# Attention and two expert layers on one core: the last pair's scalings moved ahead of the weight passes, and a woven group's relu moved ahead of the second half's exponentials

## The chip, the core and the metric

The kernel runs on one core of a Trainium2 chip. The time is the device time of one execution in microseconds (us); the less, the better. The engines that matter are TensorE (PE: matmuls, PEld: loads of their stationary operand), VectorE (DVE), ScalarE (ACT) and SyncE's queue of transfers (SP). Each engine runs its instructions in program order and waits on semaphores of the others.

## What is computed

Three steps follow each other. The attention has 2 batches x 12 heads of 448 rows with 64 columns, and its mask makes it causal. The two layers after it work on 896 tokens, 768 wide inside the model and 2048 wide in the middle.

```python
scores = scale * np.matmul(q, k.transpose(0, 1, 3, 2))
scores = np.where(mask, -1000000000.0, scores)
scores = scores - np.max(scores, axis=-1, keepdims=True)
attn = np.exp(scores)
attn = attn / (np.sum(attn, axis=-1, keepdims=True) + 1e-09)
attn_out = np.matmul(attn, v)
...
h = np.maximum(x @ w_in, 0.0)        # first layer, x from attn_out
x = (h * h @ w_out)
...
h = x @ w_in                         # second layer
g = h - np.tanh(h)
out = (g @ w_out)
```

## The kernel before, in words

**Number format.** The weights come as 64-bit words. Each unit of weights (128 x 768) is turned into two 32-bit parts by steps that alternate between engines. DVE shifts (L115), ACT scales the upper words (L105), DVE merges (L120) and sets the sign (L125), ACT rounds the result to the upper part (L127), and DVE takes the difference as the lower part (L134 or L136, in turn). After this last step, called split, SP loads the unit three further on (L98), since there are three raw buffers. The split results go into a ring of 8 buffers. Each product of the layers is then three matmuls: upper x upper, upper x lower, lower x upper (L370, L371, L372). Only the third reads the lower part of the weights.

**Attention.** The 24 heads are done as 12 pairs (`NPAIR`), numbered 0 to 11. The loop over `s` is a software pipeline: in step `s`, pair `s` gets its scores, row maxima (DVE, L296 and L298) and exponentials (ACT, L305); pair `s-1` gets the reciprocals of its row sums (DVE, `recips`) and the first of its scalings (DVE, `norms`, L317); and pair `s-2` gets the rest of its scalings, its transposes (PE, L323), the copies of these out of PSUM (ACT, `tcopy`, L329) and the product with V (PE, `pv`, L341). The result of pair `s-3` is taken out of PSUM by ACT (`xhi`, L354) and DVE (`xlo`, L358). The seven row blocks of a pair, 0 to 6, are 64 to 448 columns wide. Scores and exponentials come in two halves; `exps(s, e1[:-1])` are the exponentials of the second half. A pair's transposes go in four groups, 0 to 3, through two PSUM buffers, so that groups 2 and 3 can only be written once ACT has copied groups 0 and 1. In steps 12 and 13 there are no scores left, only the last pairs.

**Woven groups.** From step 8 on the first batch of pairs is complete, and each step weaves one group of the first layer's matmuls (18 matmuls into one PSUM buffer `h`, called from `fill`) between the attention's. There are six (`EARLY`), in steps 8 to 13, for weight units 0 to 5. At the end of its step `relus` turns the group into its activation: ACT computes relu out of PSUM (L387), squares (L388) and rounds to the upper part (L380). In the next step `relu_lows` has DVE take the lower part (L383). There is one buffer `h` for these groups: the next group cannot start before the relu has read the last one.

**Order.** The order on each engine is the order of the code. The steps of the weight preparation lie in a list `todo`; `one()` takes the next one if the budget of the step (`budget`, in nanoseconds of DVE time) is not used up, and `pump()` takes as many as the budget allows. What they leave for ACT is kept back in `act_late` and put out by `late()`. In steps 12 and 13 the budget is `SHARE_LAST`. After the loop come the rest of the first layer and the second, the weight passes, paced by other budgets.

Of the kernel before, what the change touches and what calls it, by code (L numbers as in the profile page):

```python
# [14 lines left out]
AF = mybir.ActivationFunctionType  # L15
# [12 lines left out]
NPAIR = B * NP  # L28
# [6 lines left out]


SHARE_PAIR = (800, 3300)
SHARE_LAST = 6000
SHARE_HIDDEN = (2400, 500)
SHARE_OUT = 4000  # L40

# [23 lines left out]
def body(ctx: ExitStack, tc: tile.TileContext, qT, kT, vL, w1, w2, w3, w4, out):  # L65
    nc = tc.nc
# [12 lines left out]
    def tmp(name, which="t"):  # L79
        return sb.tile([P, S], F32, tag=f"tmp{which}", bufs=4 if which == "t" else 3, name=name)  # L80
# [72 lines left out]
    def room():  # L153
        i = len(taken) - RING
        return i < 0 or taken[i] < freed[0]
# [10 lines left out]
    def late():  # L166
        while act_late:
            act_late.pop(0)()

    def one():  # L170

        if todo and budget[0] > 0 and (room() or not todo[0][3]):
            take()
            return True

    def take():
        f, cost, _, _ = todo.pop(0)
        f()
        budget[0] -= cost
# [6 lines left out]
    def pump():  # L186
        while one():
            pass
# [29 lines left out]
    def warm(count):  # L218
        o = ps.tile([P, 512], F32, tag="h", bufs=1, name="warm")[:, :S]
        for _ in range(count):  # L220
            nc.tensor.matmul(o, lhsT=ones[:, :P], rhs=ones, start=True, stop=True)
# [6 lines left out]
    for j in range(2):  # L228
        for i in range(2):
            r = maskb[D * j : D * j + D, i]  # L230
# [32 lines left out]
    def scores(n, t):  # L263
        q, k = qk[n]
        banks = []
        for z, cs in enumerate(step(n, t)):
            bank = ps.tile([P, 512], F32, tag="s", bufs=4, name=f"s{n}_{t}_{z}")
            banks.append(bank)
            for c in cs:
                sc[n, c] = bank[:, SOFF[c] : SOFF[c] + D * (c + 1)]  # L270
        for i in range(2):
            for z, cs in enumerate(step(n, t)):
                for c in cs[i : i + 1]:
                    for j in range(2):
                        r, e = slice(D * j, D * j + D), D * (j ^ z)
                        nc.tensor.matmul(sc[n, c][e : e + D], lhsT=q[r, D * c : D * c + D], rhs=k[r, : D * (c + 1)], start=(c == cs[0]), stop=False, skip_group_check=True)  # L276
        for z, cs in enumerate(step(n, t)):
            d = [SOFF[c] // D + c for c in cs]
            o = banks[z].rearrange("p (b k) -> p b k", k=D)[:, d[0] : d[-1] + 1 : max(d[-1] - d[0], 1)]
            for j in range(2):  # L280
                r, e = slice(D * j, D * j + D), D * (j ^ z)
                nc.tensor.matmul(o[e : e + D], lhsT=identb[r, r], rhs=maskb[r, : len(cs)], start=False, stop=True, skip_group_check=True)
        if t == 1:
            qk.pop(n)
            load_qk(n + 3)

    def blocks(n, t):
        return [c for cs in step(n, t) for c in cs]

    def maxes(n, t):  # L290
        if t == 0:
            stat[n] = sb.tile([P, 3, 8], F32, tag="stat", bufs=4, name=f"st{n}")
        st = stat[n]
        cs = blocks(n, t)
        for c in reversed(cs):
            nc.vector.tensor_reduce(out=st[:, 0, SI[c] : SI[c] + 1], in_=sc[n, c], axis=AX.X, op=ALU.max, negate=True)  # L296
        a, z = SI[cs[0]], SI[cs[-1]] + 1
        nc.vector.tensor_scalar_mul(out=st[:, 0, a:z], in0=st[:, 0, a:z], scalar1=0.125)  # L298

    def exps(n, cs):  # L300
        st = stat[n]
        for c in cs:
            w = D * (c + 1)
            i = SI[c]
            nc.scalar.activation(prob[n % 3][:, POFF[c] : POFF[c] + w], sc.pop((n, c)), AF.Exp, bias=st[:, 0, i : i + 1], scale=0.125, accum_out=st[:, 1, i : i + 1])  # L305

    def recips(n):
        st = stat[n]
        nc.vector.tensor_scalar_add(out=st[:, 1, :NQ], in0=st[:, 1, :NQ], scalar1=1e-9)
        nc.vector.reciprocal(out=st[:, 2, :NQ], in_=st[:, 1, :NQ])  # L310

    def norms(n, cs):
        st = stat[n]
        for c in cs:
            i = SI[c]
            p = prob[n % 3][:, POFF[c] : POFF[c] + D * (c + 1)]
            nc.vector.tensor_scalar_mul(out=p, in0=p, scalar1=st[:, 2, i : i + 1])  # L317

    def transposes(n, t):
        bank = tb[n, t] = ps.tile([P, 512], F32, tag="t", bufs=2, name=f"t{n}_{t}")  # L320
        for i, (kc, c) in enumerate(TBLK[4 * t : 4 * t + 4]):
            o = bank.rearrange("p (i j q) -> p i j q", j=2, q=D)[:, i, :: -1 if c in TURNED else 1]
            nc.tensor.transpose(o, prob[n % 3][:, POFF[c] + P * kc : POFF[c] + P * kc + P], ident)  # L323

    def tcopy(n, t):
        if t == 0:
            pt[n] = slot(3 + n % 2, [P, 16, P], F32, f"pt{n}")
        bank = tb.pop((n, t))
        nc.scalar.copy(out=pt[n][:, 4 * t : 4 * t + 4], in_=bank.rearrange("p (i q) -> p i q", q=P))  # L329
# [22 lines left out]
    def xhi(n):  # L352
        b, hp = divmod(n, NP)
        nc.scalar.copy(out=x[hp][:, 0, b], in_=ob[n][:, :S])  # L354

    def xlo(n):
        b, hp = divmod(n, NP)
        nc.vector.tensor_sub(out=x[hp][:, 1, b], in0=ob.pop(n)[:, :S], in1=x[hp][:, 0, b])  # L358
# [20 lines left out]
    def hi_of(dst, v):  # L379
        nc.scalar.copy(out=dst[0], in_=v)  # L380
# [4 lines left out]
    def relu2(h, dst):  # L385
        r = tmp("r")
        nc.scalar.activation(r, h, AF.Relu)  # L387
        nc.scalar.activation(r, r, AF.Square)  # L388
        hi_of(dst, r)
        return r  # L390
# [72 lines left out]
    def early(count):  # L463
        for m in range(count):
            dst = gdst(0, 0, m, 0)
            h = ps.tile([P, 512], F32, tag="h", bufs=1, name=f"h{m}_0")[:, :S]
            for k, _ in enumerate(first_pieces(0, 0, m, 0, h)):
                if k == KD - 1:
                    done.append((h, dst))
                yield  # L470

    done = []
    lows = []
    early_groups = early(EARLY)

    def fill(count):
        for _ in range(count):
            next(early_groups, None)

    def relus():  # L480
        while done:
            h, dst = done.pop(0)
            lows.append((dst, relu2(h, dst)))

    def relu_lows():
        while lows:
            lo_of(*lows.pop(0))
# [34 lines left out]
    for s in range(NPAIR + 2):  # L522
        p, a = s - 1, s - 2
        ss, sp, sa = s < NPAIR, 0 <= p < NPAIR, a >= 0
        f = s - 2 >= NP
        if ss:
            budget[0] = min(budget[0], 0) + (SHARE_PAIR[f] if s > 1 else 0)
            e0, e1 = blocks(s, 0)[::-1], blocks(s, 1)
        else:
            budget[0] = min(budget[0], 0) + SHARE_LAST  # L530
        if sp:
            exps(p, blocks(p, 1)[-1:])
        if ss:
            scores(s, 0)
        if sa:
            norms(a, (3, 5, 6))
        if a >= 1:
            xhi(a - 1)
        if f:
            relu_lows()  # L540
            one()
            fill(1)
        if sa:
            transposes(a, 0)
            tcopy(a, 0)
            transposes(a, 1)
            tcopy(a, 1)
        late()
        if f:
            fill(2)  # L550
        if ss:
            maxes(s, 0)
        if a >= 1:
            xlo(a - 1)
        if f:
            one()
        if ss:
            exps(s, e0[:2])
        if sp:
            recips(p)  # L560
            norms(p, (0, 1, 2))
        if f:
            one()
        if ss:
            scores(s, 1)
        if f:
            fill(1)
        if sa:
            transposes(a, 2)
            tcopy(a, 2)  # L570
            transposes(a, 3)
            tcopy(a, 3)
        if f:
            fill(2)
        late()
        if ss:
            exps(s, e0[2:])
            maxes(s, 1)
            exps(s, e1[:-1])
        if sp:  # L580
            norms(p, (4,))
        relus()
        one()
        if f:
            one()
        if sa:
            pv(a, range(4))
        if not ss:
            pump()
        late()  # L590
        if s == 1:
            warm(5)
        if s in (2, 3):
            w_load(s - 1)
        if s == 4:
            load_v(1)
# [58 lines left out]
```

## Time and profile before

| | us |
|---|---|
| runs shown | 565.03, 567.02, 1904.64 (median 567.02) |
| the profiled execution | 565.34 |
| its span, first to last instruction | 563.5 |
| PE busy | 551.8 (98%) |
| PEld busy | 482.3 (86%) |
| DVE busy | 403.8 (72%) |
| ACT busy | 337.1 (60%) |

The third run lies far off the other two; it is used for nothing but the median. The span is the time between the first and the last instruction of the profiled execution; what lies around it (1.84 us) is start and end. A busy PE is not a PE at its peak, since matmuls overlap in the records; what counts is whether it waits, and for whom. Start times are counted from the start of the span.

### The profile page before, as it was taken

Reading aid. Unit: us, or ns where it says so; the run is one execution under the profiler, and the core shown is the slowest. Engines: PE = TensorE matmul, PEld = TensorE weight load, DVE = VectorE, ACT = ScalarE, POOL = GpSimd, SP = SyncE. Lnnn points to the kernel's source line nnn. Section 1 sums busy time; section 2 is a strip of 40 time slices with the busy share of each in tenths; the row PEclk is TensorE's granted clock in tenths of the full one; section 3 lists DMA queues with packets and bytes.
Section 4 is the critical chain, followed back from the end, with each engine's and each line's share of the span. In section 5 each row is a group of like instructions: output and inputs, shape, how many; then the busy total and the mean of one; then the engine's idle time right before and its main releaser. Section 6 shows DMA issues by size and latency. Waiting matters only on the chain.

```text
span 563.5 us, 8049 instructions
## 1 busy us (share of the span) xinstructions
PE 551.8 (98%) x3134; PEld 482.3 (86%) x3134; DVE 403.8 (72%) x727; ACT 337.1 (60%) x650; POOL 1.8 (0%) x11
## 2 busy tenths in 40 slices
PE   7999999899999999999999999999999999999997
PEld 3667776699999999999999999999999999999996
DVE  5999988658564447555749489998888499889611
ACT  4999888658543238666325278776565487864200
POOL 1000000000000000000000000000000000000000
PEclk9999999899999999999999999999999999999999
DMA  8643412415342324333223330110665311015211
GB/s 292 235 150 106 147 57 82 142 57 168 113 169 94 131 61 163 112 113 112 72 97 116 109 113 1 56 58 15 209 223 176 120 42 56 1 57 173 94 49 49
DMA packets 15525, 61.85 MB, mean 110 GB/s; under 512 B 1664, under 2 KB 6400, under 8 KB 15488
## 3 DMA queue, kind: packets, MB, share of 16 engines
q1 hardware_dynamic: 15200, 61.00, 32.3%
q8 instruction: 24, 0.39, 0.3%
q10 hardware_dynamic: 288, 0.34, 0.2%
q14 instruction: 13, 0.11, 0.1%
HBM read 58.59 MB, written 2.75 MB: 109 GB/s over the span
## 4 chain that ended last, share of the span: by engine, by line
PE 83%; DVE 11%; ACT 2%; DMA 2%; SPq 1%; issue 0%; DVEq 0%; ACTq 0%
PE o L370 14%; PE o L371 14%; PE o L372 14%; PE h L370 13%; PE h L371 13%; PE h L372 13%; DVE st L296 4%; DVE p L317 2%; DMA k<-kT 2%; PE t L323 1%; ACT p L305 1%; DVE raw L120 1%; DVE x L358 1%; PE o L341 1%; DVE w L136 1%; PE s L276 1%
## 5 line engine op out<-in xcount | busy, mean ns | idle before, releaser
L370 PE MATMUL o<-g,w 128*128 128x448 f32 x384 | 140.4, 366 | 0.0
L371 PE MATMUL o<-g,w 128*128 128x448 f32 x384 | 140.4, 366 | 0.0
L372 PE MATMUL o<-g,w 128*128 128x448 f32 x384 | 140.1, 365 | 0.0
L370 PEld LDWEIGHTS o<-g,w 128*128 128x128 f32 x384 | 72.1, 188 | 6.0
L372 PEld LDWEIGHTS o<-g,w 128*128 128x128 f32 x384 | 72.1, 188 | 6.0
L371 PEld LDWEIGHTS o<-g,w 128*128 128x128 f32 x384 | 72.1, 188 | 5.8
L127 ACT CAST w<-raw 128x768 fp32r<-128x768 f32 x64 | 58.3, 911 | 30.6 <-DVE raw L125 30.6
L370 PE MATMUL h<-x,w 128*128 128x448 f32 x192 | 73.2, 381 | 2.4 <-ACT r L387 2.4
L105 ACT ACTIVATE raw<-raw 128x768 f32<-128x768 f32 x64 | 59.4, 928 | 24.4 <-DMA raw<-w 24.4
L371 PE MATMUL h<-x,w 128*128 128x448 f32 x192 | 70.8, 369 | 0.0
L372 PE MATMUL h<-x,w 128*128 128x448 f32 x192 | 70.7, 368 | 0.0
L372 PE MATMUL h<-y,w 128*128 128x448 f32 x192 | 70.6, 368 | 0.0
L371 PE MATMUL h<-y,w 128*128 128x448 f32 x192 | 70.6, 367 | 0.0
L370 PE MATMUL h<-y,w 128*128 128x448 f32 x192 | 70.6, 367 | 0.0
L125 DVE SCALAR_TENSOR_TENSOR raw<-raw 128x768 int32<-128x768 int32 x64 | 61.2, 957 | 1.2
L120 DVE SCALAR_TENSOR_TENSOR raw<-raw 128x768 int32<-128x768 int32 x64 | 61.0, 953 | 0.0
L136 DVE TENSOR_TENSOR w<-raw,w 128x768 fp32r<-128x768 f32 x32 | 30.6, 957 | 31.6 <-ACT w L127 31.5
L305 ACT ACTIVATE p<-s,st 128x128 f32<-128x128 f32 (+6 forms) x84 | 41.2, 530 | 11.1 <-DVE st L298 9.8
L383 DVE TENSOR_TENSOR g<-r,g 128x448 fp32r<-128x448 f32 x32 | 20.0, 625 | 35.7 <-ACT g L380 35.6
L134 DVE SCALAR_TENSOR_TENSOR w<-w,raw 128x768 fp32r<-128x768 f32 x32 | 30.6, 957 | 18.6 <-ACT w L127 18.5
L370 PEld LDWEIGHTS h<-x,w 128*128 128x128 f32 x192 | 36.3, 189 | 6.7 <-ACT r L387 2.8
L372 PEld LDWEIGHTS h<-x,w 128*128 128x128 f32 x192 | 36.2, 189 | 3.4
(57 smaller groups left out, 750.6 us busy)
## 6 DMA issues: line engine op xcount, KB each, us to landing
raw<-w SPq DMA_DIRECT2D x64, 768.0 KB, 4.3
q<-qT SPq DMA_DIRECT2D x12, 224.0 KB, 4.9
k<-kT SPq DMA_DIRECT2D x11, 224.0 KB, 4.1
out<-part SPq DMA_DIRECT2D x11, 224.0 KB, 1.9
v<-vL SPq DMA_DIRECT2D x2, 1152.0 KB, 6.9
vend<-vL SPq DMA_DIRECT2D x1, 384.0 KB, 8.9
k<-kT ACTq DMA_DIRECT2D x1, 224.0 KB, 3.6
out<-part ACTq DMA_DIRECT2D x1, 112.0 KB, 1.7
```

Source lines behind the costliest of these rows:

```text
L105: nc.scalar.activation(h, h, AF.Copy, scale=2.0**-112)
L120: nc.vector.scalar_tensor_tensor(out=lo, in0=hi, scalar=3, in1=lo, op0=ALU.logical_shift_left, op1=ALU.bitwise_or)
L125: nc.vector.scalar_tensor_tensor(out=lo, in0=hi, scalar=-0x80000000, in1=lo, op0=ALU.bitwise_and, op1=ALU.bitwise_or)
L127: act_late.append(lambda: nc.scalar.copy(out=st["w"][:, 0], in_=lo.bitcast(F32)))
L134: nc.vector.scalar_tensor_tensor(out=w[:, 1], in0=w[:, 0].bitcast(F32), scalar=-(1.0 - 2.0**-24), in1=f, op0=ALU.mult, op1=ALU.add)
L136: nc.vector.tensor_sub(out=w[:, 1], in0=f, in1=w[:, 0])
L296: nc.vector.tensor_reduce(out=st[:, 0, SI[c] : SI[c] + 1], in_=sc[n, c], axis=AX.X, op=ALU.max, negate=True)
L305: nc.scalar.activation(prob[n % 3][:, POFF[c] : POFF[c] + w], sc.pop((n, c)), AF.Exp, bias=st[:, 0, i : i + 1], scale=0.125, accum_out=st[ ...
L370: nc.tensor.matmul(h, lhsT=hi, rhs=xh, start=(k == 0), stop=False)
L371: nc.tensor.matmul(h, lhsT=hi, rhs=xl, start=False, stop=False)
L372: nc.tensor.matmul(h, lhsT=lo, rhs=xh, start=False, stop=(k == kk - 1))
L383: nc.vector.tensor_sub(out=dst[1], in0=v, in1=dst[0])
```

## The change

It has two parts.

In the steps that have scores and a woven group (8 to 11), the relu of the group is put out ahead of the second half's maxima and exponentials. Square and rounding stay behind the exponentials.

In step 12 the scalings of pair 11, the last one, are all put out in one piece right behind its reciprocals, where before three stood there, one a little later and three at the start of step 13. In steps 12 and 13 some of the calls that take weight preparation are left out, and the budget `SHARE_LAST` falls from 6000 to 3300, so that fewer preparation steps stand in these two steps and more behind them.

```diff
-SHARE_LAST = 6000
+SHARE_LAST = 3300
...
     def relus():
         while done:
             h, dst = done.pop(0)
-            lows.append((dst, relu2(h, dst)))
+            r = tmp("r")
+            nc.scalar.activation(r, h, AF.Relu)
+            highs.append((dst, r))
+
+    def squares():
+        while highs:
+            dst, r = highs.pop(0)
+            nc.scalar.activation(r, r, AF.Square)
+            hi_of(dst, r)
+            lows.append((dst, r))
...
-        if sa:
+        if sa and a < NPAIR - 1:
             norms(a, (3, 5, 6))
...
         if f:
             relu_lows()
-            one()
+            if ss:
+                one()
             fill(1)
...
-        if f:
+        if f and ss:
             one()
...
             recips(p)
-            norms(p, (0, 1, 2))
+            norms(p, (0, 1, 2) if ss else (0, 1, 2, 3, 4, 5, 6))
...
             exps(s, e0[2:])
+        relus()
+        if ss:
             maxes(s, 1)
             exps(s, e1[:-1])
-        if sp:
+        if sp and ss:
             norms(p, (4,))
-        relus()
+        squares()
```

On ACT, step 10, from the last copy of transposes (`pt`, pair 8) to the rounding of the woven group: `p` are the exponentials' outputs, `s_1` the scores of the second half, `h` the woven group's PSUM buffer, `r` its relu, `g` the activation.

```order
 L329 COPY pt_1089<-t_3_1144 128x512
 L305 ACTIVATE p_123,st_1103<-s_0_0_1061,st_1103 128x448
+L485 ACTIVATE r<-h_0_1080 128x448
 L305 ACTIVATE p_123,st_1103<-s_1_0_1120,st_1103 128x256
 L305 ACTIVATE p_123,st_1103<-s_1_0_1120,st_1103 128x192
 L305 ACTIVATE p_123,st_1103<-s_1_1_1121,st_1103 128x320
-L387 ACTIVATE r<-h_0_1080 128x448
-L388 ACTIVATE r<-r 128x448
+L491 ACTIVATE r<-r 128x448
 L380 CAST g_0_0_1_1079<-r 128x448
```

The relu has moved past three exponentials; steps 8, 9 and 11 show the same.

On DVE in the kernel before, from the third scaling of pair 11 (`p_124`) in step 12 to its last one in step 13: `raw` and `w` are weight units in preparation (`raw_1110` and `w_1372` are unit 6, `raw_1231` is unit 7). Ahead of these rows stand a shift of unit 6 and the lower part of unit 5 (`w_1292`, L134).

```order
L317 TENSOR_SCALAR p_124<-p_124,st_1224 128x192
L120 SCALAR_TENSOR_TENSOR raw_1110<-raw_1110 128x768
L317 TENSOR_SCALAR p_124<-p_124,st_1224 128x320
L125 SCALAR_TENSOR_TENSOR raw_1110<-raw_1110 128x768
L115 TENSOR_SCALAR raw_1231<-raw_1231 128x768
L136 TENSOR_TENSOR w_1372<-raw_1110,w_1372 128x768
L120 SCALAR_TENSOR_TENSOR raw_1231<-raw_1231 128x768
L125 SCALAR_TENSOR_TENSOR raw_1231<-raw_1231 128x768
L317 TENSOR_SCALAR p_124<-p_124,st_1224 128x256
L317 TENSOR_SCALAR p_124<-p_124,st_1224 128x384
L317 TENSOR_SCALAR p_124<-p_124,st_1224 128x448
```

In the changed kernel, from the same scaling to the lower part of the attention's result for pair 10 (`x_71`); `g` is the lower part of step 12's woven group:

```order
L317 TENSOR_SCALAR p_124<-p_124,st_1224 128x192
L317 TENSOR_SCALAR p_124<-p_124,st_1224 128x256
L317 TENSOR_SCALAR p_124<-p_124,st_1224 128x320
L317 TENSOR_SCALAR p_124<-p_124,st_1224 128x384
L317 TENSOR_SCALAR p_124<-p_124,st_1224 128x448
L115 TENSOR_SCALAR raw_1110<-raw_1110 128x768
L134 SCALAR_TENSOR_TENSOR w_1292<-w_1292,raw_988 128x768
L120 SCALAR_TENSOR_TENSOR raw_1110<-raw_1110 128x768
L125 SCALAR_TENSOR_TENSOR raw_1110<-raw_1110 128x768
L115 TENSOR_SCALAR raw_1231<-raw_1231 128x768
L383 TENSOR_TENSOR g_0_0_2_1309<-r,g_0_0_2_1309 128x448
L358 TENSOR_TENSOR x_71<-o_1373,x_71 128x448
```

The seven scalings of pair 11 now stand together. The six preparation steps that stood between them have moved behind them or further on, and so have the two that stood ahead of them, the lower part of unit 5 among them.

On ACT in the kernel before, from the rounding of step 12's woven group to the copies of pair 11's transposes (`pt`):

```order
L380 CAST g_0_0_2_1310<-r 128x448
L127 CAST w_1372<-raw_1110 128x768
L105 ACTIVATE raw_1336<-raw_1336 128x768
L127 CAST w_1389<-raw_1231 128x768
L354 CAST x_71<-o_1374 128x448
L329 COPY pt_1407<-t_0_1402 128x512
L329 COPY pt_1407<-t_1_1409 128x512
L105 ACTIVATE raw_1385<-raw_1385 128x768
L329 COPY pt_1407<-t_2_1430 128x512
```

In the changed kernel, from the same rounding (`w_1383` is unit 6):

```order
L380 CAST g_0_0_2_1309<-r 128x448
L105 ACTIVATE raw_1231<-raw_1231 128x768
L127 CAST w_1383<-raw_1110 128x768
L354 CAST x_71<-o_1373 128x448
L329 COPY pt_1398<-t_0_1393 128x512
L329 COPY pt_1398<-t_1_1400 128x512
L329 COPY pt_1398<-t_2_1419 128x512
L329 COPY pt_1398<-t_3_1425 128x512
```

Three preparation steps between the rounding and `x_71` have become two, and the one between the copies has moved behind them. PE's order is the same in both kernels.

## Rows read from the trace of the kernel before

**Rows 1.** Waits, 57 to 110 us: engine, line, waited for: us in total, times, longest
```profile
ACT p L305 <- DVE st L298: 4.0, 4, 1.3
DVE g L383 <- ACT g L380: 3.2, 3, 1.1
PE t L323 <- DVE p L317: 2.6, 1, 2.6
PE h L370 <- ACT r L387: 2.4, 3, 1.4
```

**Rows 2.** Windows: busy (xinstructions) of PE, PEld, DVE, ACT, POOL; clock, DMA share, GB/s
```profile
104.00:106.00 2.00, 2.00 (x8) 1.73 (x7) 2.00 (x5) 1.80 (x5) 0.00 (x0) 0.50 0.37 154
110.00:560.00 450.00, 450.00 (x2210) 412.82 (x2206) 308.12 (x445) 244.32 (x388) 0.00 (x0) 1.00 0.30 99
```

**Rows 3.** Chain that ended last, steps 10 and 11: start us, us, what
```profile
79.70 1.48 ACT p L305 x6
81.17 0.44 ACT r L387
81.64 0.59 ACT r L388
82.85 0.62 DVE g L383
...
91.96 0.47 PE h L370
```

**Rows 4.** Timeline of PE, last matmul of step 10's woven group: start us, us, what
```profile
77.88 0.37 PE L372 MATMUL h<-x,w 128*128 128x448 f32 x1
```

**Rows 5.** Timeline of PE, steps 12 and 13: start, duration, what [wait before]
```profile
93.47 0.45 PE L370 MATMUL h<-x,w 128*128 128x448 f32 x1
...
95.40 1.04 PE L323 MATMUL t<-ident,p 128*128 128x128 f32 x8
96.19 0.45 PE L370 MATMUL h<-x,w 128*128 128x448 f32 x1
...
100.35 0.49 PE L323 MATMUL t<-ident,p 128*128 128x128 f32 x3
103.45 1.38 PE L323 MATMUL t<-ident,p 128*128 128x128 f32 x5 [2.62 <-DVE p L317]
104.48 0.72 PE L370 MATMUL h<-x,w 128*128 128x448 f32 x1
...
107.20 1.03 PE L323 MATMUL t<-ident,p 128*128 128x128 f32 x8
```

**Rows 6.** Timeline of DVE, steps 12 and 13
```profile
94.74 0.62 DVE L358 TENSOR_TENSOR x<-o,x 128x448 fp32r<-128x448 f32 x1 [0.50 <-ACT x L354]
95.28 0.95 DVE L134 SCALAR_TENSOR_TENSOR w<-w,raw 128x768 fp32r<-128x768 f32 x1
...
96.58 0.68 DVE L317 TENSOR_SCALAR p<-p,st 128x64 f32<-128x64 f32 x3
...
98.05 0.38 DVE L317 TENSOR_SCALAR p<-p,st 128x320 f32<-128x320 f32 x1
98.34 0.97 DVE L125 SCALAR_TENSOR_TENSOR raw<-raw 128x768 int32<-128x768 int32 x1
...
103.05 1.04 DVE L317 TENSOR_SCALAR p<-p,st 128x256 f32<-128x256 f32 x3
```

**Rows 7.** Timeline of ACT, steps 12 and 13
```profile
94.60 1.08 ACT L329 COPY pt<-t 128x512 f32<-128x512 f32 x2
...
103.17 0.91 ACT L127 CAST w<-raw 128x768 fp32r<-128x768 f32 x1 [1.37 <-DVE raw L125]
...
104.41 1.07 ACT L329 COPY pt<-t 128x512 f32<-128x512 f32 x2
```

**Rows 8.** DMA issues of the weights: count, KB each, median us to landing
```profile
raw<-w SPq DMA_DIRECT2D x64, 768.0 KB, 4.3
```

More of the change, by code (lines that the diff above doesn't have):

```diff
@@ L472, in body @@
     done = []
+    highs = []
     lows = []
```

## The prediction, made before the changed kernel was run

> **What bounds the kernel now.** I read first the windows, to see where PE waits at all. From 110 to 560 us PE is busy without a gap, at a granted clock of 1.00, while DVE works 308 of 450 us and ACT 244 [rows 2]: in the weight passes nothing but PE's own matmuls counts, and a change that shortens nothing there can only let them start earlier. So I went to the waits of the stretch before, 57 to 110 us, where the change lies. PE waits there for two things that the change touches: 2.4 us in three waits for the relu that frees the woven group's PSUM buffer, and 2.6 us in one wait for scalings, ahead of transposes [rows 1]. The chain of waits shows what is behind the first: DVE's last maxima of a step release three exponentials (79.70), behind them stand relu (81.17), square (81.64) and the rounding, and these release DVE's lower part at 82.85, for which DVE waits [rows 3]; from there DVE works through to the next maxima. DVE waits so three times, 3.2 us in all [rows 1]. The second is seen in PE's timeline: of pair 11's transposes three run at 100.35, the fourth waits 2.62 us for a scaling [rows 5], and DVE does that scaling at 103.05 only, behind weight preparation [rows 6].
>
> **Part 1, the relu.** No work is added or removed; four relus move past three exponentials each. From the relu's start to the square's start the chain has 81.64 - 81.17 = 0.47 us [rows 3]. Taken out, it brings the lower part 0.47 us nearer to the maxima. DVE waits 3.2 / 3 = 1.07 us there [rows 1], so it can use all of it: three waits, 3 x 0.47 = 1.41 us, by which DVE and ACT are ahead in step 12. The relu now runs ahead of the exponentials, where ACT waits for the maxima: 4.0 us in four waits, the longest 1.3 [rows 1]. The relu's 0.44 us fits, even into the mean of the waits left, (4.0 - 1.3) / 3 = 0.9. Its input is there in time too: the group's last matmul ends at 77.88 + 0.37 = 78.25, and the exponentials start at 79.70 [rows 3, 4].
>
> PE's own gain is bounded from above by its 2.4 us of waiting and from below by nothing, if something else stops it at once. I take a value between, from what is late next: in step 12 the third group of transposes started at 95.40, and the buffers for it and the fourth are freed by ACT's two copies from 94.60 to 95.68 [rows 5, 7]. The second of them ended about 0.1 us before the fourth group wrote there (95.40 plus half of the 0.79 us that two groups take, 95.79). ACT comes 1.41 us earlier, so PE comes 1.41 + 0.1 = **1.5 us** earlier, and the other 0.9 us of its 2.4 become waits for norms and copies. Queued behind the relu on ACT are the exponentials; if the relu had to wait, they would too (a rival, below).
>
> **Part 2, the scalings of pair 11.** PE's matmuls are the same, so two like stretches can be compared. In step 12 two groups of transposes take 96.19 - 95.40 = 0.79 us; in step 13, with the wait in them, 104.48 - 100.35 = 4.13. That is 3.34 us too much, 2.62 of it the wait, the rest slow transposes. The nine matmuls behind take 95.40 - 93.47 = 1.93 us in step 12 and 107.20 - 104.48 = 2.72 in step 13 [rows 5], 0.79 too much, with a granted clock of 0.50, the lower of the two levels (1.2 GHz), from 104 to 106 [rows 2]. PE had just waited 2.62 us; behind its shorter waits for the relu the matmuls ran at full speed. So this part can give 3.34 + 0.79 = **4.13 us**, if the wait goes entirely; if a new wait takes its place, less, down to nothing.
>
> Does it go? `x_70` on DVE stood at 94.74 behind a wait for ACT [rows 6], and comes at 94.74 - 1.41 = 93.33. The reciprocals took 96.58 - 95.28 less one L134; from `x_70` to the first scaling it is 96.58 - 94.74 - 0.87 = 0.97 us without that L134 (0.95 long, some 0.08 of it overlapped, as 94.74 to 95.28 is 0.54 for an instruction of 0.62). The scalings start at 94.30 and take 0.68 + 0.38 + 1.04 = 2.10 us [rows 6]: all done by 96.4. The transposes want them at 100.35 - 1.5 = 98.85. The wait is gone, with 2.4 us to spare.
>
> What is late next: DVE's preparation behind the scalings. Shift (about 0.5), the lower part of unit 5 (0.95), merge (0.97) and sign (0.97) of unit 6 follow; with 0.08 of overlap at each of the seven joints, sign ends at 96.4 + 3.4 - 0.5 = 99.3. The lower part of unit 5 is done 1.8 us before, at 97.5; PE reads it first in the matmul just ahead of the transposes, at about 98.6. Then ACT: the rounding of unit 6 waits for that sign, and behind it stand `x_71` and the copies of pair 11. From that rounding to the first copy it was 104.41 - 103.17 = 1.24 us, and each copy takes half of 1.07 [rows 7]: the copies end at 101.1 and 101.6. PE wants the buffers at 107.20 - 1.5 - 4.13 = 101.57 and, half of 0.79 later, at 101.96. That fits with 0.4 us to spare, and is the tightest place of the new order; with no overlap at DVE's joints it would be 0.1 us late. I take no loss.
>
> **What is put off** (the smaller budget, the calls left out) is 2 x 2.7 = 5.4 us of DVE's work by the budget. I cost it at nothing: behind 110 us DVE has 450 - 308 = 142 us idle [rows 2], and by the order of the changed kernel both are level again at the lower part of unit 8. That unit is first read when the layer's second product begins, and before it stand ten groups of 18 matmuls, at 1.93 / 9 = 0.21 us each 38 us [rows 5]. The load of unit 8 is issued behind the lower part of unit 5, at 97.5 in place of 96.2, and lands 4.3 us later [rows 8], at 101.8; DVE shifts it after two more preparation steps of unit 7 and the lower part of unit 6, past 103. Without this cover PE would stand for a unit's four DVE steps, about 3.5 us.
>
> **The sum.** 1.5 + 4.13 = 5.6 us. On the profiled execution's 565.34 that is 559.7. The two runs and this one (565.03, 567.02, 565.34) have a mean of 565.8, and the median shown is 1.7 above the profiled one; from the mean I forecast 565.8 - 5.6 = **560.2 us**.
>
> **The rivals.**
>
> *A, only the scalings pay.* Something other than the relu holds the woven steps: DVE has only 1.07 us of waiting per step, and PE's matmuls could find the norms or the copies late from the first step on. For it: PE has less slack in these steps than the page's busy shares say, as the tightness of 0.1 us at 95.79 shows. Against it: DVE's wait is twice the 0.47 that are taken out. Time: 565.8 - 4.1 = 561.7.
>
> *B, a new wait for the copies of pair 11.* The rounding of unit 6 stands ahead of them on ACT and waits for DVE. For it: the same pattern cost ACT a wait of 1.37 us before [rows 7]; my slack is 0.4. It decides as soon as DVE's preparation ends 0.4 us later than I put it. If ACT's copies come as late behind the transposes' start as 104.41 - 100.35 = 4.06 us, that is at 98.85 + 4.06 = 102.9 with the first done at 103.4, PE loses 103.4 - 101.57 = 1.9 us. Time: 560.2 + 1.9 = 562.1.
>
> *C, slower: the relu blocks ACT.* Where the woven group's last matmul is late, the relu waits for it and the three exponentials behind it wait too; DVE then gets the row sums late, and each of steps 8 to 11 grows. It decides when the group ends later than the maxima less the relu, 79.70 - 0.47 = 79.23, which is 0.98 us later than now (78.25); each us beyond costs a us in each of four steps. For 4.1 us of loss, which would eat part 2 as well, it must end 2 us later than now. With 3 us later it is 4 x 2 = 8 us: 565.8 - 4.1 + 8 = 569.7. Against it: PE's group comes earlier in the new kernel, as its wait for the buffer goes. The Trainium skill says of the order that it depends on (TensorE: Matmul & The Clock Gate, in the part on the array of 32x32 sub-arrays) that ScalarE and VectorE take their queue strictly first in, first out, while only PE pulls weight loads ahead; by that no exponential can pass a waiting relu. The trace agrees as far as it goes: at 103.17 the copies stood behind a rounding that waited 1.37 us [rows 7].
>
> *D, faster by over 2%.* Would need 11 us. The waits of PE that the change touches are 2.4 + 2.6 us and the slow clock behind them 1.5, in all 6.5 [rows 1, 5]. Nothing in the rows gives more.
>
> **How the numbers follow.** Forecast 0.70, with its own range 558.8 to 562.0 (a gain of 5.0 to 6.2, since the slack that I chose between the bounds may be 0.6 off, on runs of 565.0 to 567.0); A 0.13; B 0.12; C 0.03; D 0.02. The range reaches from all 6.5 us on the fastest run, 565.03 - 6.5 = 558.5, to B with some of A, 563.0; what is left out is C, D and the ends of A and B on a slow run. A measurement of this kernel can tell about 2% from no change, 555.7 to 578.4 around the median. The forecast, A and B all lie within: same 0.95; faster 0.02; slower 0.03.
>
> **What would show it.** In the profile of the changed kernel the wait of PE for scalings ahead of transposes (2.6) is gone, the granted clock stays at 1.00 from 90 us on, and the waits for the relu are gone. The three waits of DVE for the lower part shrink from 1.07 to about 0.6. PE enters the weight passes 5.6 us earlier, and the rest of the span is as long as it was. The prediction is wrong if PE then waits for ACT's copies of pair 11 (B), if ACT's exponentials start later behind the maxima than before (C), or if PE waits behind 110 us for a unit's lower part.

## The result and the profile after

The changed kernel takes 560.16 us (median of four runs, 559.44 to 562.27). Its runs stand to those of the kernel before at 0.9889, with a 95% interval of 0.9863 to 0.9914. (That comparison has a fourth run of the kernel before, 569.43 us.) The forecast was 560.2.

The profiled executions say less at first sight: their spans are 563.5 and 560.5 us, only 3.0 apart. So I cut each span in three, at the first matmul of the first woven group and at the first matmul of the weight passes. Here are these two matmuls in PE's timeline (start us, us, engine, line, what), first of the kernel before:

```profile
51.34 0.47 PE L370 MATMUL h<-x,w 128*128 128x448 f32 x1
...
111.42 0.47 PE L370 MATMUL h<-x,w 128*128 128x448 f32 x1
```

and of the changed kernel:

```profile
54.48 0.47 PE L370 MATMUL h<-x,w 128*128 128x448 f32 x1
...
108.36 0.47 PE L370 MATMUL h<-x,w 128*128 128x448 f32 x1
```

| profiled execution | woven part starts | stretch to the weight passes | rest of the span |
|---|---|---|---|
| before | 51.34 | 60.08 | 452.08 |
| changed | 54.48 | 53.88 | 452.14 |

The stretch that the change is about is **6.20 us** shorter, and the rest is the same. The start was 3.14 us later in this execution; the last experiments are about that.

The waits of the changed kernel between 55 and 110 us (engine, line, waited for: us in total, times, longest):

```profile
ACT p L305 <- DVE st L298: 2.3, 4, 0.8
DVE g L383 <- ACT g L380: 1.5, 3, 0.5
...
PEld t L323 <- ACT pt L329: 0.6, 1, 0.6
...
PE t L323 <- ACT pt L329: 0.2, 1, 0.2
PEld t L323 <- DVE p L317: 0.2, 1, 0.2
```

Both of PE's waits in [rows 1] are gone. What it still waits for are copies, 0.2 us; its weight loads (PEld) wait 0.6 us for copies and 0.2 us for scalings of pair 10. DVE's three waits for the lower part fell from 3.2 to 1.5 us. Its timeline shows the step lengths between them and, behind the last, the scalings of pair 11 in one row:

```profile
74.85 0.62 DVE L383 TENSOR_TENSOR g<-r,g 128x448 fp32r<-128x448 f32 x1 [0.49 <-ACT g L380]
...
84.57 0.62 DVE L383 TENSOR_TENSOR g<-r,g 128x448 fp32r<-128x448 f32 x1 [0.50 <-ACT g L380]
...
94.28 0.63 DVE L383 TENSOR_TENSOR g<-r,g 128x448 fp32r<-128x448 f32 x1 [0.49 <-ACT g L380]
...
96.84 1.93 DVE L317 TENSOR_SCALAR p<-p,st 128x64 f32<-128x64 f32 x7
```

The steps are 84.57 - 74.85 = 9.72 and 94.28 - 84.57 = 9.71 us long. In the kernel before the same instructions stand 10.30 us from the one at 82.85 [rows 3] on either side:

```profile
72.55 0.62 DVE L383 TENSOR_TENSOR g<-r,g 128x448 fp32r<-128x448 f32 x1 [1.07 <-ACT g L380]
...
93.15 0.63 DVE L383 TENSOR_TENSOR g<-r,g 128x448 fp32r<-128x448 f32 x1 [1.08 <-ACT g L380]
```

On ACT the relu runs in the wait ahead of the exponentials (80.68), and square follows these directly (83.36). Further on in the same timeline stand the rounding of unit 6 and the copies of pair 11:

```profile
80.68 0.54 ACT L485 ACTIVATE r<-h 128x448 f32<-128x448 f32 x1
82.00 0.47 ACT L305 ACTIVATE p<-s,st 128x256 f32<-128x256 f32 x1 [0.77 <-DVE st L298]
...
83.36 0.58 ACT L491 ACTIVATE r<-r 128x448 f32<-128x448 f32 x1
...
102.01 0.92 ACT L127 CAST w<-raw 128x768 fp32r<-128x768 f32 x1 [0.66 <-DVE raw L125]
...
103.26 1.09 ACT L329 COPY pt<-t 128x512 f32<-128x512 f32 x2
```

PE in steps 12 and 13, to be read beside [rows 5]:

```profile
96.36 1.14 PE L323 MATMUL t<-ident,p 128*128 128x128 f32 x8 [0.23 <-ACT pt L329]
97.26 0.45 PE L370 MATMUL h<-x,w 128*128 128x448 f32 x1
...
101.42 1.03 PE L323 MATMUL t<-ident,p 128*128 128x128 f32 x8
102.21 0.45 PE L370 MATMUL h<-x,w 128*128 128x448 f32 x1
...
104.13 1.03 PE L323 MATMUL t<-ident,p 128*128 128x128 f32 x8
```

Pair 11's transposes run through in 102.21 - 101.42 = 0.79 us, and the nine matmuls behind them in 104.13 - 102.21 = 1.92. From the first of these transposes to the third group it was 107.20 - 100.35 = 6.85 us and is 2.71: 4.14 us less. The granted clock behind them, 0.50 before (104 to 106 us) [rows 2], is 1.00:

```profile
102.00:104.00 2.00, 2.00 (x14) 1.86 (x12) 1.58 (x4) 1.99 (x4) 0.00 (x0) 1.00 0.80 313
104.00:106.00 2.00, 2.00 (x15) 1.87 (x14) 1.97 (x4) 1.42 (x3) 0.00 (x0) 1.00 0.12 22
```

### The profile page after: what moved, and what is told of

The parts are those of the page before. It is cut to its first block, busy times and chain, and to the rows that moved or that the text cites. A ratio compares the mean times of both kernels' runs of the same rounds, so it can differ in the third digit from the quotient of the medians.

```text
span 560.5 us, 8048 instructions
## 1 busy us (share of the span) xinstructions
PE 551.5 (98%) x3134; PEld 482.3 (86%) x3134; DVE 403.9 (72%) x727; ACT 336.6 (60%) x650; POOL 1.8 (0%) x11
## 4 chain that ended last, share of the span: by engine, by line
PE 84%; DVE 12%; ACT 2%; DMA 1%; issue 0%; DVEq 0%; ACTq 0%
PE o L370 14%; PE o L371 14%; PE o L372 14%; PE h L370 13%; PE h L371 13%; PE h L372 13%; DVE st L296 4%; DVE p L317 3%; ACT p L305 1%; PE s L276 1%; PE o L341 1%; PE t L323 1%; DVE raw L120 1%; DVE x L358 1%; DMA k<-kT 1%; DVE st L298 1%
## 5 line engine op out<-in xcount | busy, mean ns | idle before, releaser
L134 DVE SCALAR_TENSOR_TENSOR w<-w,raw 128x768 fp32r<-128x768 f32 x32 | 30.6, 958 | 18.7 <-ACT w L127 18.5
L370 PEld LDWEIGHTS h<-x,w 128*128 128x128 f32 x192 | 36.1, 188 | 4.1
L371 PEld LDWEIGHTS h<-y,w 128*128 128x128 f32 x192 | 36.1, 188 | 3.4
```

Of the source, the lines that this page charges most:

```text
L134: nc.vector.scalar_tensor_tensor(out=w[:, 1], in0=w[:, 0].bitcast(F32), scalar=-(1.0 - 2.0**-24), in1=f, op0=ALU.mult, op1=ALU.add)
L370: nc.tensor.matmul(h, lhsT=hi, rhs=xh, start=(k == 0), stop=False)
L371: nc.tensor.matmul(h, lhsT=hi, rhs=xl, start=False, stop=False)
```

## The experiments

All stretches are read as above, from the profiled execution of each kernel. The medians and ratios are against runs of the kernel before on the same chip; its medians were 566.8, 566.5 and 566.7 us in the three sessions.

| kernel | woven part starts | stretch | against 60.08 | median us | ratio, 95% interval |
|---|---|---|---|---|---|
| relu alone | 53.51 | 58.12 | -1.96 | 565.16 | 0.9952 (0.9926 to 0.9978) |
| all of part 2 | 52.10 | 55.93 | -4.15 | 561.84 | 0.9928 (0.9902 to 0.9954) |
| of part 2, scalings in one piece only | 51.94 | 60.67 | +0.59 | 566.45 | 0.9988 (0.9976 to 1.0001) |
| of part 2, smaller budget and fewer calls only | 52.13 | 56.40 | -3.68 | 562.48 | 0.9923 (0.9908 to 0.9937) |
| wait filled with matmuls | 51.97 | 59.13 | -0.95 | 564.90 | 0.9979 (0.9960 to 0.9998) |
| late group, relu first | 51.22 | 58.71 | -1.37 | 563.85 (one run) | |
| late group, relu last | 51.78 | 56.02 | -4.06 | 561.71 (one run) | |
| changed kernel again | 55.61 | 53.90 | -6.18 | 559.78 | 0.9871 (0.9843 to 0.9900) |
| changed, first loads in another order | 51.18 | 53.89 | -6.19 | 559.46 | 0.9876 (0.9843 to 0.9909) |
| the same, and copies first | 51.17 | 53.36 | -6.72 | 558.55 | 0.9847 (0.9822 to 0.9872) |

The rest of the span was between 452.07 and 452.17 us in all of them.

**The two parts apart.** Part 1 alone keeps everything of the kernel before but the relu's place:

```diff
             exps(s, e0[2:])
+        relus()
+        if ss:
             maxes(s, 1)
...
-        relus()
+        squares()
```

(`relus` and `squares` are those of the change.)

> Part 1 of the change alone: the relu ahead of the second half's exponentials, the last pair's scalings, the budget and the calls as before. Theory of the prediction: the woven steps get shorter, by 0.47 us each in three steps by the prediction's sum, so 1.5 us off the time before; by the trace of the changed kernel, whose three steps are 0.6 to 0.7 us shorter, 2.0 us. PE's wait for the scalings ahead of pair 11's transposes stays at 2.6 us, since what stands ahead of those scalings on DVE only starts earlier. Rival (only the scalings pay): no change, 0 us.

The stretch is 1.96 us shorter. The wait for the scalings stays, as PE's timeline of this kernel shows; what stands before it has only moved forward:

```profile
103.59 1.38 PE L323 MATMUL t<-ident,p 128*128 128x128 f32 x5 [2.66 <-DVE p L317]
```

Part 2 alone takes the rest of the diff and puts the relu back:

```diff
-        relus()
         if ss:
             maxes(s, 1)
             exps(s, e1[:-1])
         if sp and ss:
             norms(p, (4,))
+        relus()
         squares()
```

> Part 2 of the change alone: the last pair's scalings in one piece, the smaller budget and the calls left out; the relu behind the exponentials as before. Theory of the prediction: 4.1 us off the time before, 3.3 from the transposes with their wait and 0.8 from matmuls at the lower clock; PE's three waits for the relu stay at 2.4 us. Rival (a new wait for the copies of pair 11 takes its place): about 2 us off.

The stretch is 4.15 us shorter. In its waits (55 to 112 us) the relu still stands, with 2.4 us on PE and 2.8 us on its weight loads:

```profile
PEld h L370 <- ACT r L485: 2.8, 3, 1.5
PE h L370 <- ACT r L485: 2.4, 3, 1.4
```

1.96 + 4.15 = 6.11, against 6.20 for both: the parts add up.

**What in part 2 does it.** Two kernels each do one half of it, on top of the kernel before. The first only puts the scalings together:

```diff
-        if sa:
+        if sa and a < NPAIR - 1:
             norms(a, (3, 5, 6))
...
-            norms(p, (0, 1, 2))
+            norms(p, (0, 1, 2) if ss else (0, 1, 2, 3, 4, 5, 6))
...
-        if sp:
+        if sp and ss:
             norms(p, (4,))
```

> Of part 2 only the scalings of the last pair in one piece behind the reciprocals; the budget (6000), the calls and the relu as before. Theory (the rival of a wait for the copies, which the smaller budget keeps away): PE's wait for scalings is gone, but the roundings of units 6 and 7 now both stand ahead of pair 11's result and copies on ACT, the second one waiting for DVE's sign of unit 7 at about 103.9; the copies end near 105.7 and 106.2, PE wants them at 103.1 and 103.5, so a wait of about 2.7 us comes back and 1.4 us of the 4.1 are left, or less if the clock falls again. Rival (the place of the scalings is what counts): 4.1 us off.

It gains nothing, where 1.4 us were expected to be left unless the clock fell again. PE's wait for scalings is gone, and a wait for copies of 2.92 us has come in its place, two groups of transposes later. ACT and PE in their timelines:

```profile
104.83 0.91 ACT L127 CAST w<-raw 128x768 fp32r<-128x768 f32 x1 [2.04 <-DVE raw L125]
105.65 0.53 ACT L354 CAST x<-o 128x448 fp32r<-128x448 f32 x1
106.08 1.08 ACT L329 COPY pt<-t 128x512 f32<-128x512 f32 x2
```

```profile
106.72 1.14 PE L323 MATMUL t<-ident,p 128*128 128x128 f32 x8 [2.92 <-ACT pt L329]
```

The rounding of unit 7 stands on ACT ahead of pair 11's result and copies, and waits 2.04 us for DVE's preparation. The clock then fell too; windows of this kernel:

```profile
108.00:110.00 2.00, 2.00 (x8) 1.32 (x8) 0.57 (x1) 1.19 (x4) 0.00 (x0) 0.50 0.53 151
```

That is the mechanism of rival B, with the rounding of unit 7 where B had that of unit 6. Its price is greater than the 1.9 us that I gave B: against all of part 2 it is 0.59 + 4.15 = 4.74 us, since the wait alone is 2.92 us and the matmuls behind it ran at the lower clock. The second kernel only prepares less, and leaves the scalings in three places:

```diff
-SHARE_LAST = 6000
+SHARE_LAST = 3300
...
             relu_lows()
-            one()
+            if ss:
+                one()
...
-        if f:
+        if f and ss:
             one()
```

> Of part 2 only the smaller budget and the calls left out; the last pair's scalings in three places as before, and the relu as before. Theory: fewer preparation steps stand ahead of the last three scalings, and these start at about 100.25, just as PE wants the first of them (100.65); waits of 0.1 to 0.4 us remain and 3.8 us come off the time before. Rival (the place of the scalings is what counts): PE's wait stays near 2.6 us and nothing comes off.

It alone brings 3.68 of the 4.15 us. DVE reaches the last three scalings at 101.08, and PE starts the transposes at 101.13 without a wait that the profile lists; they only run 0.45 us slower than free ones (1.48 against 1.03):

```profile
101.08 1.04 DVE L317 TENSOR_SCALAR p<-p,st 128x256 f32<-128x256 f32 x3
```

```profile
101.13 1.48 PE L323 MATMUL t<-ident,p 128*128 128x128 f32 x8
```

So the scalings in one piece are worth 0.47 us where less preparation stands in these steps, and nothing where it does not. The smaller budget and the calls left out were not tried apart.

**The price of the clock.** The kernel before, with 13 matmuls that nothing reads in place of the wait:

```diff
+        if s == NPAIR + 1:
+            o = ps.tile([P, 512], F32, tag="s", bufs=4, name="keep")[:, :S]
+            for _ in range(13):
+                nc.tensor.matmul(o, lhsT=ones[:, :P], rhs=ones, start=True, stop=True)
         if sa:
             transposes(a, 0)
```

> The kernel before with 13 bf16 matmuls of 128x448 that nothing reads, on PE just ahead of pair 11's first transposes, to fill the wait of 2.62 us; no part of the change. Theory (1.5 us of the 4.1 were not the wait but the lower clock behind it): the granted clock stays at 1.00, the nine matmuls behind take 1.93 us and not 2.72, the transposes still end when the scalings do, so 0.8 to 1.0 us come off the stretch from the first woven matmul to the weight passes (60.08 us before). Rival (the wait is all, the matmuls behind are slow for another reason): 0 us off, or longer by what the 13 matmuls take beyond the wait.

PE's timeline and the windows of this kernel:

```profile
100.96 2.67 PE L546 MATMUL keep<-const-bfloat16-1.0 128*128 128x448 bf16 x13
103.47 1.72 PE L323 MATMUL t<-ident,p 128*128 128x128 f32 x8
104.95 0.45 PE L370 MATMUL h<-x,w 128*128 128x448 f32 x1
...
106.88 1.03 PE L323 MATMUL t<-ident,p 128*128 128x128 f32 x8
```

```profile
104.00:106.00 2.00, 1.90 (x10) 1.52 (x11) 2.00 (x6) 2.00 (x4) 0.00 (x0) 1.00 0.74 307
```

The clock stays at 1.00, the nine matmuls take 106.88 - 104.95 = 1.93 us, and the stretch loses 0.95 us. No scaling has moved: DVE's instruction behind them starts 52.65 us after the first woven matmul, against 52.66 in the kernel before. So 2.72 - 1.93 = 0.79 us were the clock. The other 0.16 us are the transposes, which end that much earlier. What is left of the 4.13 us I put down to the wait; that is a subtraction, not a measurement.

**Rival C, the relu that blocks ACT.** Two kernels make the woven group late: the product with V goes ahead of its last six matmuls in steps 8 to 11. One is the changed kernel with that, the other has the relu behind the exponentials again.

```diff
         if f:
+            if ss:
+                pv(a, range(4))
             fill(2)
...
-        if sa:
+        if sa and not (f and ss):
             pv(a, range(4))
```

> The changed kernel with the woven group made late: in steps 8 to 11 its last six matmuls stand behind the product with V, so the group ends about 2 us later, some 0.7 us after the maxima (82.7 against 82.0 in the changed kernel's times), and the relu, which stands first, is done 1.3 us after them. Theory of the prediction's rival C (ACT in order; each of the four steps pays): each step 1.3 us longer, the stretch 53.88 + 4 x 1.3 = 59.1 us. Other theory (the loop only shifts against PE once, PE itself does not wait for it): 53.88 + 1.3 and what PE waits for the copies, about 55.5 us.

> The same late group, but with the relu behind the second half's exponentials as before the change, and part 2 as in the changed kernel. Its exponentials cannot be held up by the relu. By rival C it is the faster one of the two, at 10.3 us a step and a stretch of 55.9 to 57 us; by the other theory it is as slow as the one with the relu first, or slower by up to 0.6 us a step.

With the relu first, ACT waits for the group and the exponentials stand behind it:

```profile
82.29 0.55 ACT L485 ACTIVATE r<-h 128x448 f32<-128x448 f32 x1 [1.75 <-PE h L372]
82.73 0.47 ACT L305 ACTIVATE p<-s,st 128x256 f32<-128x256 f32 x1
```

The lower parts on DVE come 10.57 us apart (from 74.72 on):

```profile
74.72 0.62 DVE L383 TENSOR_TENSOR g<-r,g 128x448 fp32r<-128x448 f32 x1 [2.10 <-ACT g L380]
...
85.29 0.63 DVE L383 TENSOR_TENSOR g<-r,g 128x448 fp32r<-128x448 f32 x1 [1.34 <-ACT g L380]
```

and with the relu last 10.29 us:

```profile
73.07 0.62 DVE L383 TENSOR_TENSOR g<-r,g 128x448 fp32r<-128x448 f32 x1 [1.07 <-ACT g L380]
...
83.36 0.63 DVE L383 TENSOR_TENSOR g<-r,g 128x448 fp32r<-128x448 f32 x1 [1.07 <-ACT g L380]
```

The relu first is the slower one, by 2.69 us on the stretch, so the mechanism of rival C is real. With the relu last, the late group costs next to nothing: 56.02 us, against 55.93 for part 2 alone. With the relu first it costs 58.71 - 53.88 = 4.83 us against the changed kernel, near the 4 x 1.3 = 5.2 us that were expected, but not in equal parts. By the lower part at 74.72, 3.13 us of it are there (23.50 us after the first woven matmul, against 20.37), and the next step adds 10.57 - 9.72 = 0.85. Each of these two kernels was run once. In the changed kernel the price does not arise: the relu at 80.68 is done at 81.22, ahead of the exponentials at 82.00.

**The late start.** The changed kernel once more, and the changed kernel with the first loads in another order:

> The changed kernel as it is, beside the kernel before on this chip. Theory (the 3 us by which its first profiled execution started late were not the change's): the stretch from the first woven matmul to the weight passes is 53.9 us again, the woven part starts anywhere between 51.2 and 54.5 us, and the ratio of the runs lies near 1 - 6.2 / 566 = 0.989. Rival (the change delays the start): the woven part starts near 54.5 us again.

```diff
     load_qk(1)
+    load_qk(2)
     load_v(0)
-    load_qk(2)
-    w_load(0)
...
         if s == 1:
             warm(5)
+            w_load(0)
```

> The changed kernel with the first loads in another order: q and k of pair 2 ahead of v, and the first unit of weights at the end of step 1 in place of ahead of step 0. The starts of the woven part were between 51.3 and 54.5 us in six profiled executions, with the rest of the span the same within 0.1 us, and in the late ones PE and ACT stood at 13 to 15 us for pair 2. Theory (q and k of pair 2 land late behind 2.3 MB of v and weights): the start of the woven part comes to 51.3 us or a little less, and the time falls by about 1 us in the median. Rival (it is bound by the engines or by the very first loads): no change.

The stretch of the changed kernel is 53.90 again, and its start was later still, 55.61. PE's timeline of that execution names the cause, a transfer, and its windows show the clock behind it:

```profile
15.30 1.77 PE L276 MATMUL s<-k,q 64*64 64x448 f32 x12 [2.88 <-DMA k<-kT]
```

```profile
12.00:16.00 4.00, 1.12 (x7) 0.34 (x8) 2.97 (x11) 2.85 (x12) 0.00 (x0) 0.82 1.02 372
16.00:20.00 4.00, 4.00 (x34) 2.87 (x30) 2.34 (x9) 1.48 (x5) 0.00 (x0) 0.50 0.51 183
```

With q and k of pair 2 ahead of v and the weights, the same windows read

```profile
12.00:16.00 4.00, 3.92 (x38) 2.10 (x40) 3.97 (x14) 3.17 (x14) 0.00 (x0) 1.00 1.03 372
16.00:20.00 4.00, 4.00 (x48) 2.47 (x44) 3.86 (x17) 4.00 (x15) 0.00 (x0) 1.00 0.70 220
```

and the woven part starts at 51.18. The four runs lie between 558.98 and 559.93, those of the changed kernel in its second session between 559.19 and 563.40. The median fell by only 0.3 us, between two sessions, where about 1 us was expected. Three of the ten runs of the changed kernel lie above 562 us; of the nine runs with this order, these four and the five of the next kernel, none lies more than 1 us above the fastest of its kernel. That the order removes the late starts is likely by these counts, and not shown.

**The last wait.** On top of that, the rounding of unit 5 goes behind pair 10's first two copies on ACT:

```diff
             tcopy(a, 1)
+        held[0] = False
         late()
...
-        late()
+        held[0] = s == NPAIR - 1
+        if not held[0]:
+            late()
```

(`need` also leaves out its `late()` while `held` is set.)

> The changed kernel with the first loads in the other order, and in step 12 the rounding of unit 5 behind pair 10's first two copies on ACT in place of ahead of them. Theory: PE's wait for these copies (0.2 us, and 0.6 us of weight loads) goes, the stretch falls from 53.9 to about 53.4 us, the woven part starts at 51.2 us, and the time is 0.5 us below that of the other order of loads alone (559.5), some 1.2 us below the changed kernel. Rival (the norms of pair 10 hold PE there as well): the stretch stays at 53.9.

The stretch is 53.36, 0.53 us less, and the kernel takes 558.55 us, the fastest of all: 0.9847 of the kernel before.

## Why the prediction was right, and where it was not

**What bounds it: right.** The rest of the span stayed at 452.1 us in every kernel, whatever the stretch before it did.

**Part 1: right in mechanism, undersized.** The sum had 1.5 us; PE was 2.07 us nearer in step 12 (from the first woven matmul to 97.26, against 96.19 before), and the relu alone brought 1.96. The term that was mis-sized is the relu's 0.47 us. I took it from the chain, which counts it only from the end of what ran before it, 81.17. In ACT's own timeline of before, relu and square start 0.58 us apart:

```profile
81.06 0.55 ACT L387 ACTIVATE r<-h 128x448 f32<-128x448 f32 x1
81.64 0.58 ACT L388 ACTIVATE r<-r 128x448 f32<-128x448 f32 x1
```

The steps to the third and fourth lower part became 0.58 and 0.59 us shorter. The one to the first, counted from the first woven matmul, gained 0.16, and the one to the second 0.68, where I had counted nothing and 0.47. In all DVE came 2.01 us earlier and not 1.41. That PE would use up only part of its 2.4 us, and would then be held by norms and copies, was right: its weight loads still wait 0.6 us for copies and 0.2 us for scalings, and the last experiment took 0.5 us of that away.

**Part 2: right in size, wrong in what does it.** The sum had 4.13 us, and 4.14 came. But I credited all of it to the scalings' place and none to the preparation that is put off. The half experiments say the reverse: less preparation alone brings 3.68, the scalings in one piece alone nothing. My working had both changes in one order of instructions, so its times came out; it never asked what either would do without the other. The tightest place was where I put it: the copies end at 103.80 and 104.35, and PE wants the buffers at 104.13 and, half of 0.79 later, 104.52. 0.2 to 0.3 us are to spare, where I had 0.4.

**The clock: right.** 0.79 us of the slow matmuls came back, and filling the wait without removing it gave them back too.

**What is put off: right that it costs nothing later.** PE has no wait for a unit behind the stretch, and the rest of the span did not grow.

**The rivals.** A (only the scalings pay) fell. B did not come in the changed kernel; its mechanism is what the scalings in one piece alone ran into. C is a real price that the changed kernel does not pay. The Trainium skill's sentence on which C leans (TensorE: Matmul & The Clock Gate, in the part on the array of 32x32 sub-arrays), that ScalarE's queue is strictly first in, first out, agrees with these runs: with the late group, the exponentials at 82.73 stood behind a relu that waited 1.75 us.

**The total.** That the forecast of 560.2 met the median of 560.16 so closely is in part luck, since two misses cancel. On the stretch 6.2 us came where I had 5.6. And the 565.8 us from which I took them off, a mean of three executions, lay 0.7 to 1.0 us below the medians of 566.5 to 566.8 that the kernel before had in the three later sessions.

## What to carry to other kernels

When a wait sits in the middle of a pipeline's drain, look at what else the draining engines are made to do there before you move the waiting work itself: here putting off side work removed the wait, while moving the scalings alone only handed it to the next engine. Price an instruction that leaves a chain by the distance between starts on its own engine, not by what the chain leaves for it. And cut a span at fixed events before you compare two executions; a difference of 3 us in the start hid half of the gain here.

## What the runs showed of the hardware

The first loads do not land at the same time in each execution. With the same instructions, the woven part started between 51.2 and 55.6 us; between 8 and 12 us the transfers moved 289 GB/s in the kernel before and 192 in the latest start. Why they differ stays open. In the latest start PE waited 2.88 us for a transfer and then ran at the lower clock (0.50 from 16 to 20 us, against 1.00 in the kernel before), and the woven part started 4.4 us later than in the earliest. This spread is larger than either part of the change.
